# Sliding-window attention and a SwiGLU FFN on one core: an RMS chain per block, a re-spread first group, GpSimd in program order, and four blocks' x (and three blocks' q and k) transposed on TensorE

## The chip, the cores and the metric

The kernel runs on one core of a Trainium2 chip. The metric is the time of one execution in microseconds (us), as the device measures it. A "fast" run is one in the normal state. The profile is of one execution. Its span is about 2 us shorter than the time (266.6 against 268.68 us for the kernel before).

## The reference

```python
# q, k, v: (4 batches, 8 heads, 768 positions, 64); float32
scores = q @ k.T / sqrt(64)
keep   = (key < 4) | ((query - key >= 0) & (query - key < 128))   # 4 sink keys and a window of 128
attn   = softmax(where(keep, scores, -1e9)) @ v
x      = attn as (3072 tokens, 512)
xn     = x / sqrt(mean(x*x) + 1e-6) * rms_g
g      = xn @ w_gate                                              # w_gate, w_val: 512 x 1536
out    = (g * sigmoid(g) * (xn @ w_val)) @ w_out                  # w_out: 1536 x 512
```

Tokens are handled in 24 blocks of 128; six blocks make a batch element. Four blocks make a group of 512 tokens for the FFN, so there are six groups. A group has 24 gate and value parts (four matmuls of 512 columns each, 0.86 us) and then 12 output parts. The attention of later blocks is slotted between these parts.

## The kernel before

Each engine has its own queue and takes the instructions in the order of that queue (VectorE's 7.08 us wait below, with a product behind it for which nothing was missing, shows it). TensorE and SyncE take the program's order. The order on VectorE, ScalarE and GpSimd is made by a scheduler, from its own estimate of when each thing will be ready. The parts that matter here:

```python
DMA_T_FROM = 12     # q, k of blocks from here on are transposed by DMA, issued by SyncE
DMA_X_FROM = 8      # and x of blocks from here on
FA = 8              # the first FA of 12 FFN columns of group 0 are done in halves:
                    # tokens of blocks 0, 1 first (fa), those of blocks 2, 3 later (fb)
MANUAL = {PE, SP}   # engines in program order

# GpSimd issues the loads (they cast to bf16). Blocks 8 to 23 follow the output weights:
last_load = load_wo(1)
with tc.issue_after(last_load):
    for g in range(2 * GB, NB):
        unit_load(g)                       # q, k, v of block g

def by_dma(g):
    return g >= DMA_T_FROM

def unit_sink(b):                          # sink keys of a batch element, for its blocks 1 to 5
    ks = sink.tile(...)
    nc.vector.memset(ks, 0.0)
    for hi in range(2):
        nc.vector.tensor_copy(out=ksv[...], in_=QKT[b][pr, 1, :, 0:NS])   # from its first block's k
    ...                                                                    # [cut]

def by_dve(g):                             # who masks the scores of block g
    return g < 2 * NT or g % NT == 0       # VectorE to block 11, GpSimd after (NT = 6)

# [cut] after the weighted sum of an odd block: one chain for two blocks
if u == 1 and g >= 2 and g % 2 == 1:
    later(..., lambda: unit_rms(g))        # 7 small VectorE steps on 128x2, then xr of g-1 and of g

def unit_x(g):                             # x of block g to transposed form
    if g >= DMA_X_FROM: return             # (by DMA, issued in unit_xr)
    ... 4 transposes on TensorE, a copy out of PSUM ...

# [cut] group 0: eight parts of fb with little attention between them, then
#       attention of blocks 4 to 7 crowded into the parts that follow
run(fb[:8], [...]); first = [(0, s(4)), (2, s(5)), (5, s(6)), (8, s(7)), ...]
```

The softmax here doesn't subtract the row's maximum and nothing guards it: scores larger than these inputs give would overflow.

Of the kernel before, what the change touches and what calls it, by code (L numbers as in the profile page):

```python
# [9 lines left out]
ALU = mybir.AluOpType  # L10
ACT = mybir.ActivationFunctionType
FP32 = mybir.dt.float32
# [16 lines left out]
def kernel(  # L29
# [35 lines left out]
    MS_SCALE = RSQRT_SCALE / math.sqrt(DM)  # L65
    DMA_T_FROM = 12
    DMA_X_FROM = 8
    LD = 3 * NT
    FA = 8
    MANUAL = {mybir.EngineType.PE, mybir.EngineType.SP}  # L70
    MANUAL_ALL = MANUAL | {mybir.EngineType.Activation, mybir.EngineType.DVE}

# [99 lines left out]
    with tc.manual_schedule(engines={mybir.EngineType.Pool, mybir.EngineType.DVE}):  # L172
        load_q(1)
        nc.gpsimd.affine_select(
            out=ident, in_=ident, compare_op=ALU.not_equal, fill=1.0,
            base=0, pattern=[[-1, P]], channel_multiplier=1,
        )
        nc.gpsimd.affine_select(
            out=amasks[:, 1, 0, :], in_=amasks[:, 1, 0, :], compare_op=ALU.is_ge,
            fill=NEG, base=0, pattern=[[1, P]], channel_multiplier=-1,  # L180
        )
        nc.vector.tensor_scalar(
            out=amasks[:, 1, 1, :], in0=amasks[:, 1, 0, :], scalar1=-1.0, scalar2=NEG,
            op0=ALU.mult, op1=ALU.add,
        )
        nc.vector.tensor_copy(out=amasks[:, 0, :, :], in_=amasks[:, 1, :, :])
        nc.vector.memset(amasks[0:NS, 0, :, :], 0.0)
        unit_cast(0)
        unit_cast(1)
        nc.vector.memset(gt, 0.0)  # L190
        load_k(1)
        load_v(0)
        load_v(1)
        load_w(0)
        load_q(2)
        load_k(2)
        load_w(1)
        load_q(3)
        load_v(2)
        load_k(3)  # L200
        load_v(3)
        nc.gpsimd.affine_select(
            out=sel[:, P:P + NS], in_=sel[:, P:P + NS], compare_op=ALU.not_equal,
            fill=1.0, base=0, pattern=[[-1, NS]], channel_multiplier=1,
        )
        load_w(2)
        load_w(3)
        load_q(4)
        load_w(4)
        load_k(4)  # L210
        load_w(5)
        load_v(4)
        for g in range(GB + 1, 2 * GB):
            load_q(g)
            load_k(g)
            load_v(g)
            if g == GB + 1:
                nc.gpsimd.memset(gb, 0.0)
        load_q(2 * GB)
        load_k(2 * GB)  # L220
        load_wo(0)
        last_load = load_wo(1)


    with tc.issue_after(last_load):
        for g in range(2 * GB, NB):
            unit_load(g)
# [24 lines left out]
    def by_dma(g):  # L252
        return g >= DMA_T_FROM

# [70 lines left out]

    LATER = []
    DEFER = [False]

    def later(n, f):

        if DEFER[0] and n:
            LATER.append([n, f])
        else:
            f()

    def tick():
        for e in LATER:
            e[0] -= 1
        due = [f for n, f in LATER if n <= 0]
        LATER[:] = [e for e in LATER if e[0] > 0]  # L340
        for f in due:
            f()

    PTS = {}
# [38 lines left out]
    def by_dve(g):  # L383
        return g < 2 * NT or g % NT == 0

# [20 lines left out]
    def unit_s(g):  # L406
# [17 lines left out]
        for u in range(nb):  # L424
# [14 lines left out]

            wait = 0 if not by_dve(g) else 1 if g < GB else 1 + u  # L440
            for his in [(0, 1)] if nq == 2 else [(0,), (1,)]:
                later(wait, lambda u=u, et=et, his=his: masked(u, et, his))

# [14 lines left out]
    def unit_av(g, u):  # L458
# [18 lines left out]
        if g < 2:  # L477
            PV[(g, u)] = pvv
        else:
            unit_norm(g, u, pvv)  # L480
            later(0 if g < GB else 1, lambda: unit_sq(g, u))
        if u == 1 and g >= 2 and g % 2 == 1:
            later(0 if g < GB else 1 if g < 2 * GB else 3, lambda: unit_rms(g))

# [25 lines left out]
    def unit_sq(g, u):  # L510
        if g // 2 not in MS:
            MS[g // 2] = small.tile([P, 2, 2], FP32, name="ms")
        xh = X16[g][:, heads_of(g, u), :]
        sq = xpool.tile([P, 4, D], BF16, name="sq")
        nc.scalar.activation(  # L515
            out=sq, in_=xh, func=ACT.Square, scale=MS_SCALE,
            accum_out=MS[g // 2][:, g % 2, u:u + 1],
        )

    def unit_rms(g):  # L520

        ms = MS.pop(g // 2)
        m = small.tile([P, 2], FP32, name="m")
        nc.vector.scalar_tensor_tensor(
# [3 lines left out]

        y = small.tile([P, 6, 2], FP32, name="y")
        nc.vector.tensor_scalar(  # L530
            out=y[:, 0, :].bitcast(I32), in0=m.bitcast(I32), scalar1=-0.5,
            scalar2=float(0x5f3759df - 2 ** 31), op0=ALU.mult, op1=ALU.add,
        )
        nc.vector.tensor_tensor(out=y[:, 1, :], in0=y[:, 0, :], in1=m, op=ALU.mult)
        nc.vector.tensor_tensor(
            out=y[:, 2, :], in0=y[:, 1, :], in1=y[:, 0, :], op=ALU.mult,
        )
        nc.vector.scalar_tensor_tensor(
# [10 lines left out]
        )  # L549
        for i in range(2):  # L550
            later(0 if g < GB else 1 if g < 2 * GB else 1 + i, lambda i=i: unit_xr(g - 1 + i, y[:, 5, i:i + 1]))

    def unit_xr(g, y):
        x16 = X16.pop(g).rearrange("p h d -> p (h d)")
        xr = xpool.tile([P, DM], BF16, name="xr", bufs=4)
        if g == 1:
            nc.scalar.mul(xr, x16, y)
        elif g < GB:
            nc.vector.tensor_scalar(
                out=xr, in0=x16, scalar1=y, scalar2=None, op0=ALU.mult,  # L560
            )
        else:
            nc.vector.scalar_tensor_tensor(  # L563
                out=xr, in0=x16, scalar=y, in1=gb, op0=ALU.mult, op1=ALU.mult,
            )
# [10 lines left out]
    def unit_x(g):  # L576
# [5 lines left out]
        for k0 in range(0, KTN, n):  # L582
# [8 lines left out]
            src = ps[:, 0:n * P].rearrange("p (k c) -> p k c", c=P)  # L591
            if g >= GB:
                nc.scalar.copy(out=dest, in_=src)
            elif k0 > 0 or g == 3:
                nc.vector.tensor_tensor(  # L595
# [71 lines left out]

    def step(g, p, d):

        b, t = divmod(g, NT)  # L670
        at = [p + d * i for i in range(4)]
        slots = [[], [], [], []]
        if g < NB:
# [3 lines left out]
            if t == 1:  # L677
                slots[1].append(lambda: unit_sink(b))
        if 2 * GB < g <= NB:
            slots[0].append(lambda: unit_attend(g - 1))  # L680
        if g + 2 < NB and not by_dma(g + 2):
            slots[2].append(lambda: unit_t(g + 2))
        if g + 4 < NB and by_dma(g + 4):
            slots[2].append(lambda: unit_t(g + 4))
        return [(x, u) for x, us in zip(at, slots) for u in us]

    def run(parts, slots):

        slots = sorted(slots, key=lambda e: e[0])
        for s, f in enumerate(parts):  # L690
            while slots and slots[0][0] <= s:
                slots.pop(0)[1]()
            f()
            tick()
        assert not slots

    with tc.manual_schedule(engines=MANUAL_ALL):
# [24 lines left out]
        unit_sq(1, 1)  # L722
        unit_rms(1)
        unit_warm(12)
# [6 lines left out]
            op0=ALU.mult, op1=ALU.add,  # L731
        )
        nc.sync.dma_start(
            out=gb, in_=moe_rms_g.rearrange("(o d) -> o d", o=1).to_broadcast((P, DM)),
        )

    with tc.manual_schedule(engines=MANUAL):

# [4 lines left out]
        for ft in range(FA, FTN):  # L743
# [12 lines left out]
            (5, lambda: unit_attend(3)),  # L756
            (7, lambda: unit_t1(4, 0)),
        ])
        run(fb[:8], [
            (0, lambda: unit_bias(3, 1)),  # L760
            (0, lambda: unit_sp(3, 1)),
            (0, lambda: unit_x(2)),
            (0, lambda: unit_x(3)),
            (3, lambda: unit_t1(4, 1)),
            (6, lambda: unit_t1(5, 0)),
            (7, lambda: unit_t1(5, 1)),
        ])
        first = [
            (0, lambda: unit_sink_scores(0, 4)),
            (0, lambda: unit_s(4)),  # L770
            (1, lambda: unit_t(6)),
            (2, lambda: unit_s(5)),
            (2, lambda: unit_attend(4)),
            (3, lambda: unit_t(7)),
            (5, lambda: unit_s(6)),
            (5, lambda: unit_attend(5)),
            (6, lambda: unit_t(8)),
            (8, lambda: unit_s(7)),
            (8, lambda: unit_attend(6)),
            (9, lambda: unit_sink(1)),  # L780
            (9, lambda: unit_x(4)),
            (10, lambda: unit_x(5)),
            (12, lambda: unit_attend(7)),
            (15, lambda: unit_t(9)),
            (18, lambda: unit_x(6)),
            (19, lambda: unit_x(7)),
        ]
        for G in range(NG):
            if G == 0:
                parts, slots = fb[8:], first  # L790
            else:
                parts, slots = [], []
                for ft in range(FTN):
                    parts += parts_f(G, (ft,), slice(0, GN))
                for g in range(8 if G == 1 else 4 * G + 6, min(4 * G + 10, NB + 1)):
                    p = 6 * (g - 8) if G == 1 else 9 * (g - 4 * G - 6)
                    slots += step(g, p, 1.5 if G == 1 else 2)
            for tb in range(GB):
# [35 lines left out]
```

## Time and profile before

| | before |
|---|---|
| time, median of 3 (range) | 268.76 us (266.93 to 269.2) |
| span of the profiled run, mean granted TensorE clock | 266.6 us, 0.978 |
| TensorE busy / VectorE / ScalarE / GpSimd | 243.8 / 165.7 / 140.3 / 95.2 us |
| q, k, v loads, issue to landing (median) | 8 us |

The page: busy time of each engine, then TensorE's busy share and its granted clock in tenths for each fortieth of the span (6.7 us; 9 is 90% or more), and the chain of work that ended last by engine.

```profile
span 266.6 us, 4789 instructions
...
PE 243.8 (91%) x1760; PEld 123.5 (46%) x1760; DVE 165.7 (62%) x406; ACT 140.3 (53%) x321; POOL 95.2 (36%) x128
...
PE   8989599879964999999999999998899999999994
...
PEclk9999979999995999999999999999999999999998
...
PE 65%; DVE 20%; ACT 5%; DMA 4%; issue 4%; SPq 0%; DVEq 0%; ACTq 0%
...
```

TensorE is busy 91% of the span, and its two gaps stand out as low digits: the "5" at 27 to 33 us and the "64" at 73 to 87 us. Right behind both, the granted clock falls ("7" and "5" in the lower row). The stretches of 4 us show this closer. Columns: stretch, its length, busy us of PE, weight load, DVE, ACT and POOL (with instruction counts), granted clock, DMA share (the summed time of transfers as a share of the 16 engines; it can exceed 1), GB/s.

```profile
...
28.00:32.00 4.00, 1.92 (x23) 1.25 (x21) 3.25 (x12) 2.51 (x6) 3.58 (x5) 1.00 1.69 187
32.00:36.00 4.00, 3.04 (x20) 2.01 (x19) 1.08 (x2) 1.59 (x5) 2.59 (x4) 0.65 2.06 196
76.00:80.00 4.00, 1.78 (x11) 0.70 (x10) 0.00 (x0) 1.68 (x3) 2.41 (x3) 1.00 2.29 167
80.00:84.00 4.00, 0.45 (x4) 0.27 (x4) 1.68 (x4) 0.00 (x0) 2.62 (x3) 0.62 1.69 149
84.00:88.00 4.00, 3.58 (x25) 1.66 (x23) 3.79 (x10) 1.09 (x2) 2.25 (x4) 0.52 2.51 153
...
```

From 76 to 84 us TensorE does 2.2 us of work, and after that it runs at 0.52 to 0.62 of its clock. The view of waits names who waited for whom (total us, times, longest):

```profile
...
DVE ksk L280 <- DMA qkT<-ks: 9.6, 2, 7.1
...
PE pT L418 <- DVE hT L639: 5.8, 1, 5.8
...
PE pxt L586 <- DVE xr L559: 2.8, 3, 2.0
...
```

TensorE's longest wait, 5.8 us, is for VectorE (hT is the FFN's product). VectorE itself had waited 7.1 us for a DMA at the sink copy. Its timeline shows the order (start, duration, instruction, idle before it and the releaser):

```profile
...
74.52 0.68 DVE L631 SCALAR_TENSOR_TENSOR p<-th,pg 128x512 bf16<-128x512 bf16 x1
82.28 0.50 DVE L280 COPY ksk<-qkT 64x16 bf16<-64x16 bf16 x2 [7.08 <-DMA qkT<-ks]
82.81 0.69 DVE L639 TENSOR_TENSOR hT<-p,pvl 128x512 bf16<-128x512 bf16 x1
...
```

The sink copy of block 12 stands between the two halves of an ordinary FFN step, so the product hT, for which nothing was missing, starts 7 us late. The scheduler had put the copy there. Block 12's k transpose was issued by SyncE at 74.6 us and released the copy at 82.3 us, 7.7 us later:

```profile
...
72.18 2.29 SPq L261 DMA_TRANSPOSE qkT<-qs  x1
74.59 1.37 SPq L261 DMA_TRANSPOSE qkT<-ks  x1
...
```

GpSimd issues the last load of block 13 (v) at 61.8 us; each issue keeps GpSimd about 0.88 us:

```profile
...
61.80 0.91 POOL L120 DMA_DIRECT2D v<-in_v_dram  x1
...
```

And late in the run, two xr (the normalised x) in a row on VectorE hold up the product that TensorE waits for, by 1.52 us:

```profile
...
184.65 1.41 DVE L563 SCALAR_TENSOR_TENSOR xr<-x,y,gb 128x512 bf16<-128x512 bf16 x2
...
187.50 0.39 PE L654 MATMUL po<-wo,hT 128*128 128x512 bf16 x1 [1.52 <-DVE hT L639]
...
```

### The profile page before, as it was taken

The page shows a single profiled execution, that of the slowest core. Times are in us where ns is not written, and L with a number is a line of the kernel's source. Part 1 is how long each engine was busy: PE and PEld are TensorE (multiplying, and loading weights), DVE is VectorE, ACT ScalarE, POOL GpSimd, SP SyncE. Part 2 cuts the span into 40 slices and gives each one's busy share as a digit, 9 for nine tenths or more (in the row PEclk, how much of TensorE's full clock was granted, in tenths as well). Part 3 has the DMA queues.
Part 4 walks back from the last instruction along what each step waited for, and adds up shares of the span by engine and source line. Part 5 has one row for each costly group of instructions (what it writes and reads, how often), then busy time and mean ns, then how long its engine had stood idle before and what let it go on. Part 6 is the DMA issues. An engine that isn't in the chain of part 4 may idle for free.

```text
span 266.6 us, 4789 instructions
## 1 busy us (share of the span) xinstructions
PE 243.8 (91%) x1760; PEld 123.5 (46%) x1760; DVE 165.7 (62%) x406; ACT 140.3 (53%) x321; POOL 95.2 (36%) x128
## 2 busy tenths in 40 slices
PE   8989599879964999999999999998899999999994
PEld 3566476535432444444444444443444444444441
DVE  4657857896226799826868509878218895088700
ACT  2778627976661576466646336753554531333311
POOL 8977879369865930033303100312312100000000
PEclk9999979999995999999999999999999999999998
DMA  9999999999999992355630460320330203200022
GB/s 129 140 174 191 185 176 181 187 156 154 186 182 151 149 119 59 63 118 157 61 59 0 68 178 34 62 60 1 86 112 0 42 0 80 85 35 0 0 81 79
DMA packets 108695, 26.53 MB, mean 100 GB/s; under 512 B 97792, under 2 KB 105472, under 8 KB 108672
## 3 DMA queue, kind: packets, MB, share of 16 engines
q0 software_dynamic: 80704, 13.90, 70.0%
q1 hardware_dynamic: 26928, 12.07, 19.1%
q10 hardware_dynamic: 1040, 0.26, 0.5%
q8 instruction: 14, 0.23, 0.4%
q14 instruction: 9, 0.07, 0.1%
HBM read 28.58 MB, written 6.29 MB: 131 GB/s over the span
## 4 chain that ended last, share of the span: by engine, by line
PE 65%; DVE 20%; ACT 5%; DMA 4%; issue 4%; SPq 0%; DVEq 0%; ACTq 0%
PE po L654 21%; PE pg L613 16%; PE pvl L613 14%; DVE hT L639 6%; DVE p L631 5%; DMA qkT<-ks 4%; PE pT L418 3%; DVE xr L563 3%; PE pv L466 2%; PE pw L322 2%; PE pv L470 2%; ACT et L427 2%; ACT sq L515 2%; PE pqk L235 1%; DVE et L393 1%
## 5 line engine op out<-in xcount | busy, mean ns | idle before, releaser
L613 PE MATMUL pg<-xnt,wg 128*128 128x512 bf16 (+1 forms) x320 | 75.8, 364 | 1.0 <-DVE xnt L595 0.8
L613 PE MATMUL pvl<-xnt,wv 128*128 128x512 bf16 (+1 forms) x320 | 74.6, 360 | 0.0
L626 ACT ACTIVATE th<-pg 128x512 bf16<-128x512 f32 x72 | 42.8, 600 | 49.8 <-PE pg L613 49.5
L654 PE MATMUL po<-wo,hT 128*128 128x512 bf16 x288 | 65.3, 379 | 2.9 <-DVE hT L639 2.1
L631 DVE SCALAR_TENSOR_TENSOR p<-th,pg 128x512 bf16<-128x512 bf16 x72 | 48.9, 682 | 24.0 <-ACT th L626 23.8
L639 DVE TENSOR_TENSOR hT<-p,pvl 128x512 bf16<-128x512 bf16 x72 | 49.2, 685 | 5.4 <-PE pvl L613 0.8
L395 POOL TENSOR_SCALAR_AFFINE_SELECT et<-et 128x512 bf16<-128x512 bf16 x20 | 12.6, 636 | 91.1 <-ACT et L427 83.1
L613 PEld LDWEIGHTS <-wg 128*128 128x128 bf16 x320 | 30.7, 99 | 30.2 <-issue 1.2
L613 PEld LDWEIGHTS <-wv 128*128 128x128 bf16 x320 | 31.0, 99 | 29.4 <-issue 0.6
L654 PEld LDWEIGHTS <-hT 128*128 128x128 bf16 x288 | 27.5, 98 | 35.1 <-DVE hT L639 3.6
L427 ACT ACTIVATE et<-pT 128x512 bf16<-128x512 f32 x76 | 39.6, 609 | 6.9 <-PE pT L418 6.9
L661 ACT ACTIVATE osb<-po 128x512 f32<-128x512 f32 x24 | 14.3, 597 | 40.1 <-PE po L654 40.1
L515 ACT ACTIVATE sq<-x 128x256 bf16<-128x256 bf16 x48 | 20.0, 423 | 10.9 <-DVE x L505 8.5
L500 DVE RECIPROCAL rden<-pv 128x4 f32<-128x4 f32 x48 | 7.4, 171 | 27.5 <-PE pv L470 27.3
L120 POOL DMA_DIRECT2D v<-in_v_dram x24 | 21.6, 899 | 6.7 <-DMA qs<-in_q_dram 2.3
L107 POOL DMA_DIRECT2D qs<-in_q_dram x23 | 20.7, 900 | 7.3 <-DMA wo<-in_moe_w_out_dram 2.9
L107 POOL DMA_DIRECT2D ks<-in_k_dram x23 | 20.6, 894 | 5.7 <-DMA v<-in_v_dram 3.6
L505 DVE TENSOR_TENSOR x<-pv,rden 128x256 bf16<-128x256 f32 x48 | 19.6, 421 | 0.8
L393 DVE TENSOR_TENSOR et<-et,masks 128x1024 bf16<-128x1024 bf16 (+1 forms) x22 | 13.9, 636 | 7.9 <-ACT et L427 7.9
L418 PE MATMUL pT<-qkT 64*128 64x256 bf16 (+1 forms) x168 | 12.6, 265 | 6.8 <-DVE hT L639 5.8
L563 DVE SCALAR_TENSOR_TENSOR xr<-x,y,gb 128x512 bf16<-128x512 bf16 x20 | 14.1, 746 | 0.1
L470 PE MATMUL pv<-v,et 128*128 128x65 bf16 x168 | 13.1, 196 | 0.7 <-DVE p L631 0.7
(72 smaller groups left out, 185.9 us busy)
## 6 DMA issues: line engine op xcount, KB each, us to landing
out_dram<-osb SPq DMA_DIRECT2D x24, 256.0 KB, 2.2
v<-in_v_dram POOLq DMA_DIRECT2D x24, 128.0 KB, 8.3
qs<-in_q_dram POOLq DMA_DIRECT2D x23, 128.0 KB, 8.1
ks<-in_k_dram POOLq DMA_DIRECT2D x23, 128.0 KB, 7.7
wg<-in_moe_w_gate_dram POOLq DMA_DIRECT2D x6, 256.0 KB, 8.1
wv<-in_moe_w_val_dram POOLq DMA_DIRECT2D x6, 256.0 KB, 8.4
wo<-in_moe_w_out_dram POOLq DMA_DIRECT2D x2, 768.0 KB, 10.5
osb<-in_k_dram ACTq DMA_DIRECT2D x1, 256.0 KB, 4.7
```

Source lines behind the costliest of these rows:

```text
L107: nc.gpsimd.dma_start(out=tl, in_=src[b, :, t * P:(t + 1) * P, :].rearrange("h t d -> t h d"),)
L120: nc.gpsimd.dma_start(out=V16[b][:, t, :, 0:D], in_=v[b, :, t * P:(t + 1) * P, :].rearrange("h t d -> t h d"),)
L418: nc.tensor.matmul(out=banks[u][hi][:, j * w:(j + 1) * w], lhsT=QKT[b][pr, 1, hp, t * P:(t + 1) * P], rhs=QKT[b][pr, 0, hp, t * P:t * P + ...
L427: nc.scalar.activation(out=et[:, hi].rearrange("p j n c -> p (j n c)"), in_=banks[u][hi], func=ACT.Exp, scale=inv_sqrt_d,)
L505: nc.vector.tensor_tensor(out=X16[g][:, heads_of(g, u), :], in0=pvv[:, :, 0:D], in1=RDEN.pop((g, u)).unsqueeze(2).to_broadcast((P, 4, D)), ...
L515: nc.scalar.activation(out=sq, in_=xh, func=ACT.Square, scale=MS_SCALE, accum_out=MS[g // 2][:, g % 2, u:u + 1],)
L563: nc.vector.scalar_tensor_tensor(out=xr, in0=x16, scalar=y, in1=gb, op0=ALU.mult, op1=ALU.mult,)
L613: nc.tensor.matmul(out=ps[:, i * n:(i + 1) * n], lhsT=w_sb[:, kt, ft * P:(ft + 1) * P], rhs=XNT[G][:, kt, cols], start=(kt == 0), stop=(kt ...
L626: nc.scalar.activation(out=st["th"], in_=st["pg"], func=ACT.Tanh, scale=0.5)
L631: nc.vector.scalar_tensor_tensor(out=p1, in0=st["th"], scalar=1.0, in1=st["pg"], op0=ALU.add, op1=ALU.mult,)
L639: nc.vector.tensor_tensor(out=HT[key][:, i:i + n, cols], in0=p1.rearrange("p (n c) -> p n c", n=n), in1=pvl.rearrange("p (n c) -> p n c", ...
L654: nc.tensor.matmul(out=st["po"], lhsT=HT[(G, ft // 2)][:, ft % 2, tb * P:(tb + 1) * P], rhs=wo[:, ft, :], start=(ft == 0), stop=(ft == FTN ...
```

## The change

Its intent: take TensorE's waits out of the first 90 us. The RMS chain runs per block rather than per pair. Attention of blocks 4 to 8 is spread evenly over the first group. GpSimd keeps program order, loads and masks interleaved by hand, and it masks from block 7 on. TensorE transposes x up to block 11, and q and k of blocks 12, 13 and 18. One more pair of FFN columns is done in halves (FA 10). The diff, cut to its core:

```diff
-    DMA_T_FROM = 12
-    DMA_X_FROM = 8
+    DMA_T_FROM = 14
+    DMA_X_FROM = 12
-    FA = 8
-    MANUAL = {PE, SP}
+    FA = 10
+    POOL_MASK_FROM = 7
+    MANUAL = {PE, SP, Pool}
@@ loads
+        load_q(5); load_v(4)             # a little earlier than before
-    with tc.issue_after(last_load):
-        for g in range(2 * GB, NB):
+        for g in range(2 * GB, 2 * GB + 2):
             unit_load(g)                 # 8, 9; the others from slots between the parts
@@ by_dma
-        return g >= DMA_T_FROM
+        return g >= DMA_T_FROM and g % NT > 0
@@ by_dve
-        return g < 2 * NT or g % NT == 0
+        return g < POOL_MASK_FROM or g % NT == 0
@@ after a block's weighted sum
-        if u == 1 and g >= 2 and g % 2 == 1:
-            later(..., lambda: unit_rms(g))
+        if u == 1 and g >= 2:
+            unit_rms((g,))               # 6 small steps on 128x1, then one xr
@@ step: where things of block g stand between the parts of a group
+        if 2 * GB <= g - 2 < NB:
+            slots[2].append(lambda: unit_x(g - 2))
-        if g + 4 < NB and by_dma(g + 4):
+        if g + 3 < NB and by_dma(g + 3):
+        for n in LOADS.pop(0) if LOADS else ():          # (14,15), (16,17), ... one pair a step
+            slots[1].append(lambda n=n: unit_load(n))
@@ group 0
+    FIRST = [(0, x(2)), (0, x(3)), (1, ...), (5, s(4)), (9, s(5)), (9, attend(4)), (13, s(6)), ...,
+             (16, s(7)), (20, attend(7)), (23, s(8)), (24, t(10)), (26, x(7))]
+    for g in range(10, 14):
+        FIRST.append((4 * g - 37, lambda g=g: unit_load(g)))   # loads 10 to 13: slots 3, 7, 11, 15
... cut: the deferral helpers (never switched on), the pair-and-single form of unit_sq and unit_rms,
    x of blocks 2 and 3 multiplied by the gain on VectorE, the starts of the later groups' slots
```

More of the change, by code (lines that the diff above doesn't have):

```diff
@@ L65 @@
     MS_SCALE = RSQRT_SCALE / math.sqrt(DM)
-    DMA_T_FROM = 12
-    DMA_X_FROM = 8
+    DMA_T_FROM = 14
+    DMA_X_FROM = 12
     LD = 3 * NT
-    FA = 8
-    MANUAL = {mybir.EngineType.PE, mybir.EngineType.SP}
+    FA = 10
+    POOL_MASK_FROM = 7
+    MANUAL = {mybir.EngineType.PE, mybir.EngineType.SP, mybir.EngineType.Pool}
     MANUAL_ALL = MANUAL | {mybir.EngineType.Activation, mybir.EngineType.DVE}
@@ L210 @@
         load_k(4)
+        load_q(5)
+        load_v(4)
         load_w(5)
-        load_v(4)
-        for g in range(GB + 1, 2 * GB):
+        load_k(5)
+        load_v(5)
+        for g in range(GB + 2, 2 * GB):
             load_q(g)
@@ L216 @@
             load_v(g)
-            if g == GB + 1:
-                nc.gpsimd.memset(gb, 0.0)
         load_q(2 * GB)
@@ L221 @@
         load_wo(0)
-        last_load = load_wo(1)
-    with tc.issue_after(last_load):
-        for g in range(2 * GB, NB):
+        load_wo(1)
+        for g in range(2 * GB, 2 * GB + 2):
             unit_load(g)
@@ L324, in unit_warm @@
             )
-    LATER = []
-    DEFER = [False]
-    def later(n, f):
-        if DEFER[0] and n:
-            LATER.append([n, f])
-        else:
-            f()
-    def tick():
-        for e in LATER:
-            e[0] -= 1
-        due = [f for n, f in LATER if n <= 0]
-        LATER[:] = [e for e in LATER if e[0] > 0]
-        for f in due:
-            f()
     PTS = {}
@@ L438, in masked @@
                 mask(e.rearrange("p i j n c -> p (i j) n c"), g, nq)
-            wait = 0 if not by_dve(g) else 1 if g < GB else 1 + u
             for his in [(0, 1)] if nq == 2 else [(0,), (1,)]:
-                later(wait, lambda u=u, et=et, his=his: masked(u, et, his))
+                masked(u, et, his)
     PVB = {}
@@ L480, in unit_av @@
             unit_norm(g, u, pvv)
-            later(0 if g < GB else 1, lambda: unit_sq(g, u))
-        if u == 1 and g >= 2 and g % 2 == 1:
-            later(0 if g < GB else 1 if g < 2 * GB else 3, lambda: unit_rms(g))
+            unit_sq(g, u)
+        if u == 1 and g >= 2:
+            unit_rms((g,))
     def unit_attend(g):
@@ L510, in unit_sq @@
     def unit_sq(g, u):
-        if g // 2 not in MS:
-            MS[g // 2] = small.tile([P, 2, 2], FP32, name="ms")
+        n, i = (2, g) if g < 2 else (1, 0)
+        if i == 0 and u == 0:
+            MS[g] = small.tile([P, n, 2], FP32, name="ms")
         xh = X16[g][:, heads_of(g, u), :]
@@ L516, in unit_sq, with unit_rms @@
             out=sq, in_=xh, func=ACT.Square, scale=MS_SCALE,
-            accum_out=MS[g // 2][:, g % 2, u:u + 1],
+            accum_out=MS[g - i][:, i, u:u + 1],
         )
-    def unit_rms(g):
-        ms = MS.pop(g // 2)
-        m = small.tile([P, 2], FP32, name="m")
+    def unit_rms(gs):
+        n = len(gs)
+        ms = MS.pop(gs[0])
+        m = small.tile([P, n], FP32, name="m")
         nc.vector.scalar_tensor_tensor(
@@ L527, in unit_rms @@
         )
-        y = small.tile([P, 6, 2], FP32, name="y")
+        y = small.tile([P, 6, n], FP32, name="y")
         nc.vector.tensor_scalar(
@@ L533, in unit_rms @@
         )
-        nc.vector.tensor_tensor(out=y[:, 1, :], in0=y[:, 0, :], in1=m, op=ALU.mult)
-        nc.vector.tensor_tensor(
-            out=y[:, 2, :], in0=y[:, 1, :], in1=y[:, 0, :], op=ALU.mult,
-        )
+        if n == 1:
+            nc.vector.scalar_tensor_tensor(
+                out=y[:, 2, :], in0=y[:, 0, :], scalar=y[:, 0, :], in1=m,
+                op0=ALU.mult, op1=ALU.mult,
+            )
+        else:
+            nc.vector.tensor_tensor(out=y[:, 1, :], in0=y[:, 0, :], in1=m, op=ALU.mult)
+            nc.vector.tensor_tensor(
+                out=y[:, 2, :], in0=y[:, 1, :], in1=y[:, 0, :], op=ALU.mult,
+            )
         nc.vector.scalar_tensor_tensor(
@@ L549, in unit_rms @@
         )
-        for i in range(2):
-            later(0 if g < GB else 1 if g < 2 * GB else 1 + i, lambda i=i: unit_xr(g - 1 + i, y[:, 5, i:i + 1]))
+        for i, g in enumerate(gs):
+            unit_xr(g, y[:, 5, i:i + 1])
     def unit_xr(g, y):
@@ L557, in unit_xr @@
             nc.scalar.mul(xr, x16, y)
-        elif g < GB:
+        elif g == 0:
             nc.vector.tensor_scalar(
@@ L591, in unit_x @@
             src = ps[:, 0:n * P].rearrange("p (k c) -> p k c", c=P)
-            if g >= GB:
+            if g >= 2:
                 nc.scalar.copy(out=dest, in_=src)
-            elif k0 > 0 or g == 3:
+            elif k0 > 0:
                 nc.vector.tensor_tensor(
@@ L665, in parts_o, with step @@
         return [lambda i=i: part(i) for i in range(FTN // 4)]
-    def step(g, p, d):
+    def step(g, p):
         b, t = divmod(g, NT)
-        at = [p + d * i for i in range(4)]
-        slots = [[], [], [], []]
+        slots = [[] for _ in range(7)]
         if g < NB:
@@ L677, in step @@
             if t == 1:
-                slots[1].append(lambda: unit_sink(b))
-        if 2 * GB < g <= NB:
+                slots[2].append(lambda: unit_sink(b))
+        if g <= NB:
             slots[0].append(lambda: unit_attend(g - 1))
+        if 2 * GB <= g - 2 < NB:
+            slots[2].append(lambda: unit_x(g - 2))
         if g + 2 < NB and not by_dma(g + 2):
-            slots[2].append(lambda: unit_t(g + 2))
-        if g + 4 < NB and by_dma(g + 4):
-            slots[2].append(lambda: unit_t(g + 4))
-        return [(x, u) for x, us in zip(at, slots) for u in us]
+            slots[4].append(lambda: unit_t(g + 2))
+        if g + 3 < NB and by_dma(g + 3):
+            slots[4].append(lambda: unit_t(g + 3))
+        for n in LOADS.pop(0) if LOADS else ():
+            slots[1].append(lambda n=n: unit_load(n))
+        return [(p + i, u) for i, us in enumerate(slots) for u in us]
+    LOADS = [(14, 15), (16, 17), (18, 19), (20, 21), (22, 23)]
     def run(parts, slots):
@@ L693, in run @@
             f()
-            tick()
-        assert not slots
+        while slots:
+            slots.pop(0)[1]()
     with tc.manual_schedule(engines=MANUAL_ALL):
@@ L722 @@
         unit_sq(1, 1)
-        unit_rms(1)
+        unit_rms((0, 1))
         unit_warm(12)
@@ L732 @@
         )
+        nc.vector.memset(gb[:, 0:1], 0.0)
         nc.sync.dma_start(
@@ L735 @@
         )
+    FIRST = [
+        (0, lambda: unit_x(2)),
+        (0, lambda: unit_x(3)),
+        (1, lambda: unit_t1(4, 1)),
+        (3, lambda: unit_t1(5, 0)),
+        (5, lambda: unit_sink_scores(0, 4)),
+        (5, lambda: unit_s(4)),
+        (7, lambda: unit_t1(5, 1)),
+        (9, lambda: unit_s(5)),
+        (9, lambda: unit_attend(4)),
+        (10, lambda: unit_t(6)),
+        (12, lambda: unit_t(7)),
+        (13, lambda: unit_s(6)),
+        (13, lambda: unit_attend(5)),
+        (14, lambda: unit_x(4)),
+        (15, lambda: unit_t(8)),
+        (16, lambda: unit_s(7)),
+        (16, lambda: unit_attend(6)),
+        (17, lambda: unit_sink(1)),
+        (18, lambda: unit_x(5)),
+        (19, lambda: unit_t(9)),
+        (20, lambda: unit_attend(7)),
+        (21, lambda: unit_x(6)),
+        (23, lambda: unit_sink_scores(1, 2)),
+        (23, lambda: unit_s(8)),
+        (24, lambda: unit_t(10)),
+        (26, lambda: unit_x(7)),
+    ]
     with tc.manual_schedule(engines=MANUAL):
@@ L756 @@
             (5, lambda: unit_attend(3)),
-            (7, lambda: unit_t1(4, 0)),
-        ])
-        run(fb[:8], [
-            (0, lambda: unit_bias(3, 1)),
-            (0, lambda: unit_sp(3, 1)),
-            (0, lambda: unit_x(2)),
-            (0, lambda: unit_x(3)),
-            (3, lambda: unit_t1(4, 1)),
-            (6, lambda: unit_t1(5, 0)),
-            (7, lambda: unit_t1(5, 1)),
-        ])
-        first = [
-            (0, lambda: unit_sink_scores(0, 4)),
-            (0, lambda: unit_s(4)),
-            (1, lambda: unit_t(6)),
-            (2, lambda: unit_s(5)),
-            (2, lambda: unit_attend(4)),
-            (3, lambda: unit_t(7)),
-            (5, lambda: unit_s(6)),
-            (5, lambda: unit_attend(5)),
-            (6, lambda: unit_t(8)),
-            (8, lambda: unit_s(7)),
-            (8, lambda: unit_attend(6)),
-            (9, lambda: unit_sink(1)),
-            (9, lambda: unit_x(4)),
-            (10, lambda: unit_x(5)),
-            (12, lambda: unit_attend(7)),
-            (15, lambda: unit_t(9)),
-            (18, lambda: unit_x(6)),
-            (19, lambda: unit_x(7)),
-        ]
+            (8, lambda: unit_t1(4, 0)),
+            (9, lambda: unit_bias(3, 1)),
+            (9, lambda: unit_sp(3, 1)),
+        ])
+        for g in range(2 * GB + 2, 2 * GB + 6):
+            FIRST.append((4 * g - 37, lambda g=g: unit_load(g)))
         for G in range(NG):
             if G == 0:
-                parts, slots = fb[8:], first
+                parts, slots = fb, FIRST
             else:
@@ L794 @@
                     parts += parts_f(G, (ft,), slice(0, GN))
-                for g in range(8 if G == 1 else 4 * G + 6, min(4 * G + 10, NB + 1)):
-                    p = 6 * (g - 8) if G == 1 else 9 * (g - 4 * G - 6)
-                    slots += step(g, p, 1.5 if G == 1 else 2)
+                g0, n = (9, 5) if G == 1 else (4 * G + 6, 4)
+                for g in range(g0, min(g0 + n, NB + 1)):
+                    slots += step(g, 36 * (g - g0) // n)
             for tb in range(GB):
```

## The prediction

> **What bounds it now.** TensorE. The page gives PE 243.8 us busy of a 266.6 us span (DVE 165.7, ACT 140.3, POOL 95.2); the chain of waits is 65% PE. What can be won is PE's idle time and its matmuls at reduced clock, nearly all before 90 us (stretches of 4 us):
> - 28 to 36 us: PE busy 4.96 of 8, clock 0.65 after. The second half of the first group needs x of blocks 2 and 3; their shared RMS chain waits for block 3's squares. In the timeline x transposes wait 1.99 us, the next gate 0.79; then eight gate matmuls take 1.89 us, not 0.87.
> - 48 to 60 us: PE loses about 3 us; DVE is behind.
> - 76 to 84 us: the largest. PE waits 5.8 us for DVE (waits view). DVE stands in its queue at the sink key copy of block 12, which waits 7.1 us for a DMA transpose (2.4 us at quiet times, 7.66 here among block loads). The clock falls to 0.52 to 0.62 until 88 us: about 1.9 us more.
> - After 100 us only some 4.6 us are idle (longest 1.5 us at 184, behind two xr of 0.70 us on DVE).
>
> The Trainium skill, "TensorE: Matmul & The Clock Gate", section "The HAM clock gate", says that an idle window of about 3.4 us halves the clock; this trace agrees (0.52 after the 5.8 us wait).
>
> **What the change does.**
> 1. Blocks 12 and 18 are transposed by PE (13 too), so the sink copy waits for ACT instead of a crowded DMA: removes 5.8 + 1.9 us on the critical path. Gain 7.5.
> 2. Two more parts of the first half (FA 10; 1.73 us of matmuls) run before x of 2 and 3 is needed, and the chain is per block. Estimate: the second half starts near 33 us with those parts done; gain 2.7, about 1 us of stall left.
> 3. Attention of 4 to 8 spread over 33 to 68 us. DVE has about 19 us of work, ACT 18, for 18 us of PE before the first output matmul: still tight; gain 1.
> 4. Masks of block 7 on GpSimd stand behind the loads of block 13. Before, those were issued until 62.7 us (POOL timeline); after, PE wants the masked scores near 59 to 61 us. I expect a new stall of 2 to 4 us. Masks of 7 to 11 free DVE of about 6 us, largely off the path.
> 5. Added PE work: 40 transposes at about 0.055 us = 2.2 us, on the path. ACT: 4 copies of 0.59 and 3 of 1.01 us. DVE: 22 chains of about 1 us against 11 of 1.24, off the path after 100 us; xr come singly: saves about 1.2 us of later stalls.
>
> Sum: -7.5 -2.7 -1 +3 +2.2 -1.2 = about -7.2.
>
> **Prediction: 261.5 us, 256.5 to 267.0.** Faster by over 2% 0.66, within 2% 0.31, slower 0.03.
>
> **What would show it.** Right: no DVE wait for a DMA transpose at the sink copy; PE clock 1.00 from 72 to 90 us; second half's first gate near 33 us; first output matmul near 52 us instead of 59.9. Step 4: the first mask on POOL right behind block 13's last load, near 62 to 63 us, PE waiting for POOL at block 7's weighted sum.
>
> **What would make it wrong.** No POOL stall: 257 or less. A POOL stall over 4 us dropping the clock, loads of 14 and later held behind masks arriving late, or DVE falling behind in the first two groups: 266 or more.

## The result and the profile after

| | before | after |
|---|---|---|
| time, median of 4 (range) | 268.74 us (266.93 to 269.2) | 257.63 us (257.26 to 259.34) |
| ratio of fast runs | | 0.9611 (95%: 0.955 to 0.9673) |
| span, mean granted clock of the profiled run | 266.6 us, 0.978 | 255.3 us, 0.998 |

A ratio is the mean time of one kernel's fast runs over that of the other's fast runs in the same rounds, so it is not quite the ratio of the medians.

The same lines of the page for the changed kernel:

```profile
span 255.3 us, 4922 instructions
...
PE 240.6 (94%) x1791; PEld 125.8 (49%) x1816; DVE 168.2 (66%) x451; ACT 144.3 (56%) x326; POOL 105.3 (41%) x145
...
PE   8899889887999999999999999999999999999992
...
PEclk9999999999999999999999999999999999999999
...
PE 59%; DMA 15%; DVE 9%; POOL 8%; ACT 4%; issue 4%; POOLq 0%; DVEq 0%; ACTq 0%
...
```

The deep gaps have gone and the clock row is nines throughout. TensorE is busy 3.2 us less although it runs 56 matmuls more in the program (the counts in the page miss a few records); it no longer runs a part of them at a reduced clock (0.52 to 0.65 in the stretches shown before). The stretches of 4 us, in the columns of before:

```profile
...
28.00:32.00 4.00, 3.02 (x33) 2.19 (x30) 3.27 (x13) 2.22 (x6) 2.97 (x4) 1.00 2.02 172
32.00:36.00 4.00, 3.03 (x36) 2.48 (x31) 2.11 (x5) 2.43 (x5) 3.22 (x5) 1.00 1.81 181
60.00:64.00 4.00, 2.34 (x27) 1.27 (x25) 1.79 (x6) 2.42 (x6) 3.71 (x6) 1.00 2.19 185
76.00:80.00 4.00, 3.48 (x29) 1.54 (x28) 3.90 (x9) 2.92 (x7) 4.00 (x5) 1.00 1.51 96
80.00:84.00 4.00, 3.95 (x35) 2.17 (x35) 3.74 (x13) 3.10 (x9) 3.86 (x7) 1.00 2.46 149
84.00:88.00 4.00, 4.00 (x44) 2.19 (x42) 3.73 (x8) 2.42 (x4) 3.89 (x5) 1.00 2.00 111
...
```

Clock 1.00 everywhere, and 80 to 88 us, which held 4.03 us of TensorE work before, holds 7.95. There is a new hole at 60 to 64 us: 2.34 of 4. TensorE's own waits say for whom (line numbers moved by up to 19; L400 is what L418 was, L451 what L470 was):

```profile
...
PE pv L451 <- POOL et L377: 1.7, 2, 0.9
PE pT L400 <- ACT qkT L268: 1.4, 2, 0.8
...
PE pg L602 <- DMA wg<-in_moe_w_gate_dram: 1.0, 1, 1.0
...
```

It is GpSimd, and its timeline shows why: block 7's first mask (L377) starts right behind the last load of block 13.

```profile
...
60.41 0.91 POOL L121 DMA_DIRECT2D v<-in_v_dram  x1
61.29 0.68 POOL L377 TENSOR_SCALAR_AFFINE_SELECT et<-et 128x512 bf16<-128x512 bf16 x1
61.88 0.67 POOL L382 TENSOR_SCALAR_AFFINE_SELECT et<-et 128x512 bf16<-128x512 bf16 x1
...
```

The sink copy of block 12, the instruction that had waited 7.08 us, now waits for nothing:

```profile
...
86.75 0.45 DVE L279 COPY ksk<-qkT 64x16 bf16<-64x16 bf16 x2
...
```

To see where the 11 us came from, I took from the timeline of TensorE the time at which each group's first gate matmul starts. Differences of neighbouring starts give the length of each group:

| group | before: start, length | after: start, length | gained |
|---|---|---|---|
| first (with all the start-up) | 0, 71.66 | 0, 71.60 | 0.06 |
| second | 71.66, 48.82 | 71.60, 40.40 | 8.42 |
| third | 120.48, 38.91 | 112.00, 37.17 | 1.74 |
| fourth | 159.39, 38.82 | 149.17, 37.35 | 1.47 |
| fifth | 198.21, 33.32 | 186.52, 33.02 | 0.30 |
| sixth, to the end of the span | 231.53, 35.07 | 219.54, 35.76 | -0.69 |

In the sixth, the matmuls take the same time; the loss comes after the last of them. So the first group, in which most of the diff lives, gained next to nothing by this measure. The second group gained three quarters of the whole, and the later ones gained 2.8 us net.

The first boundary is not quite the same in both kernels. In the changed kernel the scores of block 9 and the weighted sum of block 8 (70.45 to 71.60 us on TensorE) and the q, k transposes of block 10 (67.96 to 68.41 us) stand before the second group's first gate matmul; before the change they stood behind it. That is 1.6 us of TensorE work. Like for like, I estimate from these times that the first group gained about 1.7 us and the second about 6.8. The first group's own gain is plain up to its first output matmul: 52.63 us, against 57.07 before. Of these 4.4 us the moved work takes 1.6; e4 and e6 below show where most of the rest went.

### The profile page after: what moved, and what is told of

The parts are those of the page before. It is cut to its first block, busy times and chain, and to the rows that moved or that the text cites. A ratio compares the mean times of both kernels' runs of the same rounds, so it can differ in the third digit from the quotient of the medians.

```text
span 255.3 us, 4922 instructions
## 1 busy us (share of the span) xinstructions
PE 240.6 (94%) x1791; PEld 125.8 (49%) x1816; DVE 168.2 (66%) x451; ACT 144.3 (56%) x326; POOL 105.3 (41%) x145
## 4 chain that ended last, share of the span: by engine, by line
PE 59%; DMA 15%; DVE 9%; POOL 8%; ACT 4%; issue 4%; POOLq 0%; DVEq 0%; ACTq 0%
PE po L643 21%; PE pvl L602 15%; PE pg L602 15%; DMA wg<-in_moe_w_gate_dram 10%; DMA wo<-in_moe_w_out_dram 5%; DVE p L620 3%; DVE hT L628 3%; PE pT L400 2%; ACT et L409 2%; POOL ks L108 2%; POOL qs L108 2%; POOL v L121 2%; PE pv L447 1%; PE pv L451 1%; ACT sq L497 1%
## 5 line engine op out<-in xcount | busy, mean ns | idle before, releaser
L602 PE MATMUL pg<-xnt,wg 128*128 128x512 bf16 (+1 forms) x319 | 73.7, 352 | 2.2 <-DMA wg<-in_moe_w_gate_dram 1.0
L602 PE MATMUL pvl<-xnt,wv 128*128 128x512 bf16 (+1 forms) x321 | 73.5, 352 | 0.8 <-DVE hT L628 0.5
L377 POOL TENSOR_SCALAR_AFFINE_SELECT et<-et 128x512 bf16<-128x512 bf16 x30 | 18.9, 635 | 77.0 <-ACT et L409 70.0
L552 DVE SCALAR_TENSOR_TENSOR xr<-x,y,gb 128x512 bf16<-128x512 bf16 x22 | 16.5, 749 | 0.4
L382 POOL TENSOR_SCALAR_AFFINE_SELECT et<-et 128x512 bf16<-128x512 bf16 x24 | 15.2, 635 | 0.0
L451 PE MATMUL pv<-v,et 128*128 128x65 bf16 x168 | 12.8, 194 | 1.7 <-POOL et L377 1.7
L400 PE MATMUL pT<-qkT 64*128 64x256 bf16 (+1 forms) x168 | 12.0, 261 | 1.4 <-ACT qkT L268 1.4
```

Source lines behind the costliest of these rows:

```text
L377: nc.gpsimd.affine_select(out=ev[:, :, 0, :], in_=ev[:, :, 0, :], compare_op=ALU.is_ge, fill=0.0, base=0, pattern=[[0, x], [1, P]], channe ...
L400: nc.tensor.matmul(out=banks[u][hi][:, j * w:(j + 1) * w], lhsT=QKT[b][pr, 1, hp, t * P:(t + 1) * P], rhs=QKT[b][pr, 0, hp, t * P:t * P + ...
L602: nc.tensor.matmul(out=ps[:, i * n:(i + 1) * n], lhsT=w_sb[:, kt, ft * P:(ft + 1) * P], rhs=XNT[G][:, kt, cols], start=(kt == 0), stop=(kt ...
```

## The experiments

My theories when I planned these: (A) the wait at block 12's sink copy is most of the gain; (A2) the later gain comes from single chains; (A3) the first group did gain, and gave it back at block 7's masks. The rivals are named in each expectation. "Before" was timed again in each set (medians 267.92, 268.45 and 268.33 us, against 268.74 above), so kernels of different sets (they ran on three chips) may be compared within some tenths of a per cent. The changed kernel itself was timed once, in four runs (257.26 to 259.34 us); differences of about 1 us from it are therefore weak. All runs gave correct results.

| run | median us (runs) | ratio to before | second group starts, its length |
|---|---|---|---|
| changed kernel | 257.63 (4) | 0.9611 | 71.60, 40.40 |
| e1: before, blocks 12 and 13 by TensorE | 259.16 (4) | 0.9671 | 71.36, 40.78 |
| e2: changed, 12 on all by DMA | 262.73 (4; one slow; fast runs 262.55) | 0.9778 | profile slow |
| e3: changed, pair chains | 277.73 (6) | 1.0367 | 79.89, 50.30 |
| e4: changed, loads behind block 7's masks | 255.04 (6) | 0.9508 | 69.18, 40.39 |
| e5: changed, only 12 and 13 by DMA | 257.61 (6) | 0.9618 | 71.16, 42.44 |
| e6: changed, block 7 masked by VectorE | 254.15 (6) | 0.9488 | 68.81, 40.35 |
| e7: changed, FA 8 | 258.86 (6) | 0.9666 | 73.25, 40.26 |
| e8: e4 with FA 8 | 257.58 (6) | 0.9613 | 71.62, 40.27 |
| e9: e1 with FA 10 | 257.85 (6) | 0.9613 | 68.88, 40.85 |
| e10: e6 with x of 8 to 11 by DMA | 255.92 (6) | 0.9525 | 68.97, 43.35 |

### e1: one number in the kernel before

```diff
-    DMA_T_FROM = 12
+    DMA_T_FROM = 14
```

> The kernel before with one number changed: blocks 12 and 13 are transposed by TensorE instead of by DMA (DMA transposes from block 14). Theory A (the wait of VectorE for the DMA transpose of block 12 at its sink key copy cost 5.8 us of idle TensorE and about 1.9 us of reduced clock, and this is most of the gain): 260.5 to 262 us, no wait of DVE for a DMA transpose near 75 us, second group's length down from 48.8 to about 41 us. Rival B (the DMA is crowded at this time, so the wait only moves to the next thing that a transfer holds): 266 or more, with a new wait of 4 us or more between 72 and 95 us.

Measured: 259.16 us. One number gives 8.8 us of the 11.1 (its own before: 267.92). The second group shrinks from 48.82 to 40.78 us, with all other groups within 0.6 us of before. Theory A holds, and rival B falls: nothing took the wait's place. The stretches that were nearly empty before are full, at a full clock, although the DMA share is as high as it was:

```profile
...
76.00:80.00 4.00, 4.00 (x41) 2.02 (x40) 3.63 (x9) 3.08 (x7) 3.22 (x4) 1.00 2.29 170
80.00:84.00 4.00, 4.00 (x29) 1.92 (x27) 3.49 (x7) 2.95 (x8) 3.66 (x5) 1.00 2.43 155
...
```

The time is below the expected 260.5 to 262 us. The gain is 1.1 us more than the 7.7 us of wait and reduced clock that I had added up; 0.56 us of that lies in the third group, and the rest is not explained.

### e2: the changed kernel with all transposes from block 12 on by DMA

```diff
-    DMA_T_FROM = 14
+    DMA_T_FROM = 12
-        return g >= DMA_T_FROM and g % NT > 0
+        return g >= DMA_T_FROM
```

> The changed kernel with all transposes from block 12 on by DMA again (as before), all else as changed. Theory A: the scheduler places the sink key copy on VectorE right where it believes the transfer to land, early in the second group, so the wait comes back: 260 to 265 us, DVE waiting 3 us or more for the DMA transpose between 73 and 83 us. Rival C (the loads are held back behind masks in GpSimd's order, so the DMA is quiet and a transpose lands in about 2.5 us; this alone would have removed the wait): within 1 us of the changed kernel, 256.5 to 258.5 us.

Measured: 262.73 us, inside theory A's range, but for the wrong reason. The profiled run was a slow one (265.7 us; the other three 261.2 to 262.9), so I use only its order of events. At block 12 VectorE waited a mere 0.74 us. The wait sits at the other sink copy, block 18's:

```profile
...
136.37 1.20 DVE L279 COPY ksk<-qkT 64x16 bf16<-64x16 bf16 x2 [2.30 <-DMA qkT<-ks]
...
```

```profile
...
138.34 0.27 PE L433 MATMUL pv<-vsk,esk 64*128 64x260 bf16 x1 [3.59 <-DVE p L620]
...
```

The first line is VectorE's timeline, the second TensorE's: the 2.30 us wait of the copy becomes 3.59 us of idle TensorE. So a number in the expected range did not decide between the theories here, and the two blocks had to be taken apart. The next run, e5, differs from e2 in block 18 alone: its transposes on TensorE are worth about 5 us in the changed kernel (257.61 against 262.55 us). In e1 block 18 still goes by DMA and its copy waits only 1.3 us. The changed kernel issues DMA transposes three blocks ahead and not four; whether that makes the difference was not tested.

### e5: only blocks 12 and 13 by DMA

```diff
-    DMA_T_FROM = 14
+    DMA_T_FROM = 12
-        return g >= DMA_T_FROM and g % NT > 0
+        return g >= DMA_T_FROM and g != 18
```

> The changed kernel with blocks 12 and 13 transposed by DMA, block 18 by TensorE as changed. The run before this one (all by DMA) showed VectorE waiting only 0.74 us at block 12's sink copy and TensorE waiting 3.6 us at block 18's. Theory C (in the changed kernel the loads of blocks 14 and on stand behind masks, the DMA is quiet when block 12 is transposed, so block 12 no longer needs TensorE): 256.5 to 258.3 us, transposes of block 12 landing in under 3 us. Theory A (crowding at block 12 comes back): 260 us or more.

Measured: 257.61 us, the time of the changed kernel. SyncE issued block 12's transposes at 71.08 and 72.47 us, and VectorE's copy was released at 74.89, so k landed in 2.4 us (7.7 us before):

```profile
...
71.08 1.28 SPq L260 DMA_TRANSPOSE qkT<-qs  x1
72.47 1.19 SPq L260 DMA_TRANSPOSE qkT<-ks  x1
...
```

```profile
...
74.89 0.57 DVE L279 COPY ksk<-qkT 64x16 bf16<-64x16 bf16 x2 [0.74 <-DMA qkT<-ks]
...
```

Rival C holds for block 12: in the changed kernel the loads from block 14 on stand behind masks, and the DMA engines are far less busy when block 12 is transposed. The windows show the DMA share at 0.53 in 72 to 76 us, against 2.29 in 76 to 80 us of before:

```profile
...
72.00:76.00 4.00, 4.00 (x26) 2.09 (x25) 1.69 (x7) 3.48 (x10) 3.93 (x6) 1.00 0.53 109
...
80.00:84.00 4.00, 3.53 (x23) 1.77 (x23) 2.58 (x8) 1.70 (x6) 4.00 (x7) 0.57 2.56 133
...
```

It was not quite free, though: after three short waits of 0.22 to 0.61 us near 79 us the clock was 0.57 for a stretch, and the second group was 2 us longer in this profile, while the medians show no loss. The change thus removes the big wait twice over. Undoing one removal (TensorE for block 12, here) costs nothing in the medians, while e1 shows that the same one is worth 8.8 us where it is the only one. The other removal, the loads held back, was not undone by itself.

### e3: pair chains in the changed kernel

```diff
-        n, i = (2, g) if g < 2 else (1, 0)
+        n, i = (2, g % 2)
-        if u == 1 and g >= 2:
-            unit_rms((g,))
+        if u == 1 and g >= 2 and g % 2 == 1:
+            unit_rms((g - 1, g))
```

> The changed kernel with the RMS chain again once per pair of blocks (from block 2 on), all else as changed. Theory A2 (the chain per block, with single xr, is what took away the 3.2 us of later idle, in groups three and four): 259 to 260.5 us, groups three and four each 0.8 us or more longer, idle of TensorE behind two xr in a row back. Rival D (the later idle went for another reason: slots, masks, order): 257 to 258 us, groups three and four unchanged within 0.3 us. In the first group the pair chain should also delay x of block 2, up to 1 us.

Measured: 277.73 us, slower than before the change. No theory of mine had this. TensorE's waits:

```profile
...
PE pxt L575 <- DVE xr L552: 15.2, 6, 4.5
...
```

In the changed kernel TensorE transposes x up to block 11 at a fixed place in its own queue, soon after the block's weighted sum. With a pair chain the even block's xr has to wait for the odd block, TensorE stands at the transpose, and the odd block's work stands behind it. The chain for blocks 4 and 5 shows how late both xr come (VectorE's timeline: the chain's first step, then both xr):

```profile
...
54.85 0.16 DVE L507 SCALAR_TENSOR_TENSOR m<-ms 128x2 f32<-128x2 f32 x1
...
56.40 1.42 DVE L552 SCALAR_TENSOR_TENSOR xr<-x,y,gb 128x512 bf16<-128x512 bf16 x2
```

TensorE then waited 4.52 us for that xr. So the chain per block is not an extra in this kernel: the x transposes on TensorE need it. In the groups where x goes by DMA the experiment is clean: third, fourth and fifth group take 38.59, 38.57 and 33.31 us, against 37.17, 37.35 and 33.02 with single chains. That is 2.9 us for theory A2, and rival D falls. (e1, which has pair chains too, shows nearly the same three lengths: 38.35, 38.56 and 33.32 us.)

### e4: loads of blocks 12 and 13 behind block 7's masks

```diff
-            FIRST.append((4 * g - 37, lambda g=g: unit_load(g)))
+            FIRST.append((4 * g - 37 + (5 if g > 11 else 0), lambda g=g: unit_load(g)))
```

> The changed kernel with the loads of blocks 12 and 13 five parts later, so that on GpSimd the masks of block 7 stand ahead of them. Theory A3 (the rearranged first group gained 2 to 3 us and gave them back at block 7, where TensorE waits for masks that stand in GpSimd's queue behind loads): 255 to 256.5 us, first mask on POOL near 57 us rather than 61.3, the second group starts near 69.5 us rather than 71.6. Rival E (VectorE and ScalarE are full in this stage, so the wait moves to them): 257 to 258 us and the second group starts at 71 us or later.

Measured: 255.04 us, 2.6 us under the changed kernel. The first mask follows the last load of block 11 after a wait of 1.31 us, at 56.88 us in place of 61.29:

```profile
...
54.69 0.88 POOL L121 DMA_DIRECT2D v<-in_v_dram  x1
56.88 0.63 POOL L377 TENSOR_SCALAR_AFFINE_SELECT et<-et 128x512 bf16<-128x512 bf16 x1 [1.31 <-DVE x L486]
...
```

The second group starts at 69.18 us. All of the gain lies in the first group; its later lengths are those of the changed kernel. Theory A3 holds.

### e6: block 7 masked by VectorE

```diff
-    POOL_MASK_FROM = 7
+    POOL_MASK_FROM = 8
```

> The changed kernel with block 7 masked by VectorE, GpSimd from block 8. If TensorE's wait at block 7 is the queue of loads on GpSimd alone: about as good as putting the loads behind the masks, 254.8 to 256 us. If VectorE, which gets 1.4 us of masks back in its fullest stretch, is as tight as I estimated in the prediction: 256.3 us or more, with TensorE waiting for VectorE before 72 us.

Measured: 254.15 us, 3.5 us under the changed kernel, below the range I had expected, and the best of all. TensorE's longest waits with a releaser other than the start-up are now these:

```profile
...
PE pT L400 <- ACT qkT L268: 1.4, 2, 0.8
...
PE pg L602 <- ACT xnt L582: 0.7, 1, 0.7
...
```

VectorE had room for 1.4 us of masks. My estimate in the prediction that it was tight up to the first output matmul may stand, but block 7's masks come after that, where it had slack.

### e7 and e8: FA 8, with and without the wait at block 7

```diff
-    FA = 10
+    FA = 8
```

> The changed kernel with four pairs of half parts (FA 8) in place of five. Theory F (the first group's gains are swallowed, because block 7's masks cannot start before block 13's loads are issued at about 61.3 us, whatever comes before): within 0.7 us of the changed kernel, 257 to 258.3 us, with a smaller wait for POOL and a larger one for x of blocks 2 and 3. If instead FA 10 is worth its estimated 1.5 to 2 us: 259 us or more.

> The kernel with loads of blocks 12 and 13 behind block 7's masks (255.0 us), with FA 8. Theory F: here nothing swallows the first half, so FA 8 costs what FA 10 was meant to gain: 256.2 to 257.5 us, the second group starting 1.2 to 2.5 us later than 69.2 us. If FA 10 gains nothing even here: 254.5 to 255.6 us.

Measured: in the changed kernel FA 8 costs 1.2 us (258.86), between the two expectations. With the loads out of the way it costs 2.5 us (257.58, just above the expected range, against 255.04). So FA 10 earned 2.5 us, about as predicted, and the queue at block 7 swallowed half. One side effect was not separated: with FA 8 the second half has two parts more, so all units in `FIRST`, which keep their part numbers, stand two parts further ahead of the output matmuls (e9 moves its slots to avoid this). What FA 10 avoids is more than the wait itself; in e8 the clock goes too (columns as above):

```profile
...
28.00:32.00 4.00, 2.18 (x27) 1.45 (x26) 3.73 (x12) 2.87 (x7) 2.61 (x4) 1.00 1.94 171
32.00:36.00 4.00, 3.33 (x21) 2.47 (x20) 0.75 (x2) 1.18 (x2) 3.22 (x5) 0.60 1.80 181
...
```

### e9: two numbers in the kernel before

```diff
-    DMA_T_FROM = 12
-    FA = 8
+    DMA_T_FROM = 14
+    FA = 10
... the same units at the same distance from the output matmuls:
-        run(fb[:8], [..., (6, unit_t1(5, 0)), (7, unit_t1(5, 1))])
+        run(fb[:6], [..., (4, unit_t1(5, 0)), (5, unit_t1(5, 1))])
-                parts, slots = fb[8:], first
+                parts, slots = fb[6:], first
```

> The kernel before with two numbers changed: DMA transposes from block 14 (259.2 us alone) and five pairs of half parts (FA 10; slots shifted so that the same units stand at the same distance from the output matmuls). FA 10 was worth 2.5 us in the kernel with block 13's loads behind the masks. If that carries over: 256.3 to 257.5 us, the wait for x of blocks 2 and 3 down from 1.9 us to under 1 us, no reduced clock at 33 us, so that two numbers give as much as the whole change. If the pair chain for blocks 2 and 3 or VectorE holds it: 258.3 us or more.

Measured: 257.85 us (256.58 to 259.06), between the two expectations: FA 10 brings about 1.3 us here rather than 2.5, within the spread of these runs. In its profile, which is of the fastest run, the wait for x of blocks 2 and 3 fell to 0.3 us and the clock stayed up, but a wait for x of block 4 behind VectorE grew from 1.1 to 2.4 us. Two numbers give as much as the whole change; e4 and e6 show what the change as it stands loses at block 7.

### e10: x of blocks 8 to 11 by DMA again

```diff
-    DMA_X_FROM = 12
+    DMA_X_FROM = 8
```

> The kernel with block 7 masked by VectorE (254.15 us), and x of blocks 8 to 11 by DMA transposes as before. If TensorE time in the second group is all on the path, as I reckoned: the 16 transposes cost about 0.9 us, so 253.0 to 253.7 us. If the DMA transposes in this stretch of loads hold up the queue of SyncE or the start of the third group: 254.5 us or more.

Measured: 255.92 us (254.32 to 256.56), 1.8 us worse than e6 (253.9 to 254.41). The profile is of the slowest of these runs. In it three x transposes in a row on SyncE, each waiting for its own xr, hold its queue from 75 to 92.7 us, and the transposes of block 14's q and k stand behind them:

```profile
...
74.99 17.71 SPq L559 DMA_TRANSPOSE xnt<-xr  x3
92.80 1.28 SPq L260 DMA_TRANSPOSE qkT<-qs  x1
...
```

In e6 block 14's q was issued at 75.66 us, here at 92.80; it then took until 101.34 us, 8.5 us, to release TensorE, amid loads again (the DMA share was 2.92 in 96 to 100 us). TensorE waits for that q:

```profile
...
PE pT L400 <- DMA qkT<-qs: 2.2, 1, 2.2
...
```

My reckoning that taking 16 transposes off TensorE would save 0.9 us was wrong in sign for the whole: the alternative, as SyncE's queue stands here, costs more. What the transposes cost on TensorE is not shown by this.

## Why the prediction was right or wrong

The time, 257.63 us, lies in the range (256.5 to 267.0), and faster by over 2% was the most likely outcome. The predicted gain was 7.2 us and the measured one 11.1 us. Three of the marks named in the prediction came true: no wait of VectorE at block 12's sink copy, a clock of 1.00 from 72 to 90 us, and the first output matmul at 52.63 us (for before the prediction gives 59.9, but the trace has 57.07). Point by point:

1. **Sink copy (predicted 7.5 us).** Right in mechanism and nearly in size: e1 alone gained 8.8 us, 8.04 of them in the second group. What I missed is that the change removes this wait a second time, by holding back the loads (e5).
2. **FA 10 and the chain for block 2 (predicted 2.7 us).** FA 10 is right in size where nothing swallows it, 2.5 us (e8 against e4), and about half of it elsewhere (e7, e9); the chain for block 2 was not tested by itself. The second half's first gate started at 34.70 us, not near 33: the halves' last gate waited 0.98 us for weights still on their way, a wait which I had not foreseen.
3. **Spreading the attention (predicted 1 us).** Not tested by itself; it stays open, and so does the share of GpSimd's masks for blocks 8 to 11. The first group as a whole gained 0.06 us, or about 1.7 like for like.
4. **Masks of block 7 behind block 13's loads (predicted a new stall of 2 to 4 us, first mask at 62 to 63 us).** Right: the first mask was at 61.29 us, TensorE waited 1.7 us for GpSimd, and taking the stall away is worth 2.6 us (e4) or 3.5 us (e6).
5. **Added TensorE work on the path (predicted 2.2 us) and later stalls saved by single xr (predicted 1.2 us).** The second of these is the term that was mis-sized. Measured, the third to fifth group gained 3.5 us, of which single chains account for 2.9 us (e3); e1, which still has pair chains, gained 0.8 us there. What the added transposes cost is not shown. The second group holds 32 of the 40 and still gained 8.4 us, but 1.6 us of attention had left it, and TensorE is busy there for 31.29 of the 32 us from 72 to 104 us, so the added work may well cost its time. Undoing 16 of them costs 1.8 us (e10), but by way of SyncE's queue.

By stage, like for like (so with estimates for the first two groups): the first group was predicted to gain 0.7 us, from terms 2, 3 and 4, and gained about 1.7. The second gained about 6.8, where term 1 less four fifths of the added work would give about 5.7. The third to fifth gained 3.5, where 1.2 less the rest of the added work would give about 0.8. At the end, after the last output matmul, 0.7 us were lost. So the gain of every stage but the end was set too low, that of the later stalls most of all. These errors added up rather than cancelled; the stated range was wide enough to hold their sum of 3.9 us.

## What to carry to other kernels

An instruction that waits for a transfer, put early into an in-order queue, delays everything behind it: look for the wait behind the wait (TensorE on VectorE on a DMA), and first try the smallest edit that takes that operand off the transfer. When a change removes one cause in two ways, undoing one of them can show nothing (e5); test each alone on the kernel before as well. And when a stage that was reworked shows no gain, check first whether work was moved across its boundary (1.6 us here), and then look for one fixed event in it (here the last load issue, which ends at 61.3 us) that swallows what came before; moving that event is where the next gain lies (254.15 us here).

## What the Trainium skill lacked or had wrong

- "TensorE: Matmul & The Clock Gate", section "The HAM clock gate": it puts the fall to half clock after an idle window of about 3.4 us. Single long waits agree (0.52 after 5.8 us, and 0.56 after 4.52 us in e3). But in e5 three waits of 0.61, 0.22 and 0.53 us within 2 us were followed by 0.57, although TensorE was busy 3.11 of the 4 us that held two of them, and in e8 2.18 us busy of 4 was followed by 0.60. Before the change, too, the clock was 0.65 in the stretch behind a longest wait of 1.99 us. The page's section on a second failure mode says that frequent short idles make the clock swing as well, but it gives no measure of how many it takes.
- "DMA: Bandwidth & Descriptors", section "Anatomy of one DMA — SWDGE (gpsimd) path": it calls descriptor generation "small, variable" (its section on latency gives about 1 us to the first byte, and names this work of GpSimd's as the reason). Here each load of q, k or v holds GpSimd 0.87 to 1.01 us at its issue (median 0.90), so that the six loads of blocks 12 and 13 put a mask 4.4 us back (61.29 against 56.88 us in e4); the page does not warn that compute on GpSimd queues behind it.
- The same page, section "DMA Transpose (X-bar)": it gives no landing time. Here a 128x512 bf16 transpose takes 2.4 us at quiet times, and 7.7 us (8.5 in e10) among loads.
